# Gate and up weights loaded in eighths, transposes in quarters, the down groups regrouped, and three step counts moved

## The chip, the cores and the metric

The kernel runs on one core of one Trainium2 chip. A time is the device time of one whole execution in microseconds (us); lower is better. The profile was taken on one execution of its own. Engines are named as the profile names them: PE is TensorE (matmuls, with its weight loads as PEld), DVE is VectorE, ACT is ScalarE, POOL is GpSimd, SP is SyncE, which here issues every DMA of the program from one in-order queue.

## What is computed

One transformer layer over 2048 rows of width 512, everything in fp32, with 32 heads of width 16 that share one key and one value head, and a gated linear unit of inner width 1792:

```python
mod = (silu(c) @ w_mod).reshape(1, 6, 1, 512)       # sa, ca, ga, sb, cb, gb
h = layernorm(x) * (1 + ca) + sa
q, k, v = h @ wq, h @ wk, h @ wv                    # q: 32 heads of 16; k and v: one head of 16
o = softmax(q @ k.T / 4) @ v                        # for each head
x = x + ga * (o @ wo)
h = layernorm(x) * (1 + cb) + sb
x = x + gb * ((sigmoid(h @ w_gate) * (h @ w_up)) @ w_down)
```

Products of activations with weights are made from fp16 pairs: each fp32 operand is split into a high and a low half, and three matmuls (high by high, high by low, low by high) stand for one.

## The kernel before

**Units and half-steps.** A prologue normalizes x and makes k, v and a first part of q. Then come 32 attention units. A unit is one block `b` of 256 rows (8 blocks) and one group `o` of 8 heads (4 groups). It runs 16 steps `kb`, one for each 128 keys, and every step has two half-steps, `n` = 0 and 1; `s` = 16 times the unit plus `kb` counts steps through the program. A half-step issues, in a fixed order on PE, 8 score matmuls `sa` for a later unit (DVE takes row maxima `mx` of two 128x512 tiles from them), 8 score matmuls `st` (ACT makes two tiles `P` of exponentials) and 4 fp32 matmuls that add P times V into `craw`. After them `piece(s, n)` issues a piece of other PE work, if the plan has one: a slice of a q, wo, gate/up or down product.

**The other work.** Once the four units of a block are done, the block's feed-forward part (`ffn_block`) becomes available: one `wo` couple (attention output times wo, `wo_group`), seven gate/up couples `gu_group` (one for each chunk of 256 of the 1792 inner columns), and two down couples `down_group`. A couple is two products, one for each 128 rows, whose matmuls alternate between the two halves of PE's rows. A gate/up couple has 192 matmuls of 64x32 by 512 columns, a `piece` carries 8 or a multiple of it (mostly 16 or 24). `plan` takes the next couple from the list `work` when the last one is used up; `pick` holds the head of the list back until what it needs has been transposed (`marks`) plus `GAP` = 2 steps; `pace` sets how many terms go into a half-step, between 2 and 3 for these couples, from what is left and the steps until it is due. Nothing overtakes the head of the list. The two down couples of a block cover the 14 inner slices as 8 (`HF`) and 6, and their order in the list is: six gate/up couples, the first down couple, the seventh gate/up couple, the second down couple. The `wo` couple of a block is urgent: from step 9 of the unit that follows the block's last one it goes ahead of whatever is left in the list, once the couple under way has ended.

**The chain from wo to gate.** When a wo product ends, `norm` (deferred by 1 step for the first 128 rows and 3 for the second) adds the residual on POOL; `norm2`, 2 steps later, makes mean and variance on DVE and 7 POOL instructions of the normalization (`row_norm`); `norm3`, 1 step later, scales and shifts on POOL and splits into the pair `h2r`; 3 steps later (`HLATE`) SP issues a DMA transpose of 8 blocks of 128x128 that makes `h`, and sets the mark. Gate/up couples have a like chain: ACT (`th`) and DVE or ACT (`u`) evict, POOL makes `gr` in 4 instructions (`gated_rows`), 3 steps later (`GLATE`) SP transposes it to `g`, which the down couples read.

**Weights.** The gate and up weights are split once into fp16 pairs by `weight_jobs` (a DMA of 256 KB to `wst`, three POOL instructions) and stored to `wD` in DRAM, seven chunks of 1 MB. Jobs for wo, gate/up and the first 10 slices of w_down (42 in all) are spread over `WSTEPS` = 90 steps; the last four, whose place in SBUF the q weights hold, follow from step 100. Each gate/up couple needs its chunk back in SBUF as `gw`, of which there are two buffers; `ask` issues the load of the chunk after, one DMA of 1 MB, when a couple begins.

**Also on SP,** once in a unit: two DMAs `lD<-cs`, eight `raw<-cs`, `lc<-lD`, six `qp<-qD`, `lD<-rc` and `raw<-lD` (they carry the softmax sums to and fro and place the attention output by rows, so that POOL can make `a`, which wo reads), and four `qp<-mh`. What is pinned runs on each engine in the order in which the code issues it; only the tail, after the last unit, is ordered by a scheduler.

Of the kernel before, what the change touches and what calls it, by code (L numbers as in the profile page):

```python
# [16 lines left out]
P = 128  # L17
# [10 lines left out]
NDC = D // P  # L28
# [33 lines left out]

SKIP = 9
GAP = 2
CHAIN = 26
QRATE = 1.1
MOST = 3
# [1 line left out]
HELD = 60  # L69
SWAP = 5  # L70
FRESH = 0.9
WSTEPS = 90
WLAST = 100
WLATE = 2
WSTORE = 5
# [13 lines left out]
NCH = F // 256  # L89
# [3 lines left out]
def adaln_mqa_glu_kernel(  # L93
# [133 lines left out]
    def pair(name):  # L227
        return wp.tile([P, 2, 512], F16, tag="f16", name=name, bufs=HBUFS)
# [24 lines left out]
    sp1 = Ordered(nc.sync)  # L253
# [500 lines left out]
    now = [0]  # L754

    def defer(n, f_):
        waits.append((now[0] + n, f_))

    WO = {}
    wD = dr.tile([NCH, P, NDC, 4, 256], F16, name="wD")  # L760
    CH = [*range(2, NCH), 0, 1]
    FS = [2 * c_ + e for c_ in CH for e in range(2)]

    def gw_tile():
        return P2.tile([P, NDC, 4, 256], F16, tag="gw", name="gw", bufs=GWB)
# [26 lines left out]
    tail = []  # L792

    marks = {}

    use, gws = [0], {}

    def ask(upto):
        while use[0] <= upto:
            k = use[0]  # L800
            gws[k] = gw_tile()
            sp1.dma_start(gws[k], wD[CH[k % NCH]])
            use[0] += 1

    def ffn_block(b, end_of_all=False):
        x1, xrs, h2, ups, ths, gT = {}, {}, {}, {}, {}, {}
        at = b * NCH
        HF = 8

        def wo_group(t):  # L810
            def term(n, rs):
                o, i = divmod(n, 3)
                a_, w_ = passes(*aTs[b, o], WO['woh'], WO['wol'])[i]
                return a_[rs, t * P:(t + 1) * P], w_[rs, o, :]

            def begin():
                xrs[t] = t32("xr")
                sp1.dma_start(xrs[t], x[b * QU + t * P:b * QU + (t + 1) * P, :])

            def end(po, second):  # L820
                xr, t1 = xrs.pop(t), t32("t1")
                if second:
                    act.activation(t1, po, AF.Identity)
                    pool.tensor_tensor(t1, t1, mods[2], op=ALU.mult)
                else:
                    dve.tensor_tensor(t1, po, mods[2], op=ALU.mult)
                if tail:
                    dve.tensor_tensor(xr, t1, xr, op=ALU.add)
                    row_norm([t1], [xr])
                    dve.tensor_tensor(t1, t1, mods[4], op=ALU.mult)  # L830
                    dve.tensor_tensor(t1, t1, mods[3], op=ALU.add)
                    x1[t] = xr, t1
                else:
                    defer(1 + 2 * t, lambda: norm(t, t1, xr))

            return Group("wo", 12, "po", term, end, begin)

        def norm(t, t1, xr):
            pool.tensor_tensor(xr, t1, xr, op=ALU.add)
            defer(2, lambda: norm2(t, t1, xr))  # L840

        def norm2(t, t1, xr):
            row_norm([t1], [xr], later=True)
            defer(1, lambda: norm3(t, t1, xr))

        def norm3(t, t1, xr):
            x1[t] = xr, t1
            pool.tensor_tensor(t1, t1, mods[4], op=ALU.mult)
            pool.tensor_tensor(t1, t1, mods[3], op=ALU.add)
            rows = pair("h2r")  # L850
            pool.tensor_scalar(rows[:, 0], t1, 1.0, 0.0, op0=ALU.mult, op1=ALU.add)
            pool.tensor_tensor(rows[:, 1], t1, rows[:, 0], op=ALU.subtract)
            h2[t] = turned(rows, f"h2{t}")
            if b == 0 and t == 0:
                ask(0)
            defer(HLATE, h2[t][1])

        def turned(rows, name):
            t_ = pair(name).rearrange("p a (c r) -> p (a c) r", r=P)

            def go():
                sp1.dma_start_transpose(t_, rows.rearrange("p a n -> p (a n)"))
                marks[b, name] = now[0]

            return t_, go

        def gu_group(c_, t):
            def begin():
                if t == 0:
                    ask(at + c_ + 1)  # L870
                    ths[c_], ups[c_] = t32("th"), t32("u")

            def term(n, rs):
                k, i = divmod(n, 3)
                gw = gws[at + c_]
                h_, w_ = ((0, 0), (1, 0), (0, 1))[i]
                return h2[t][0][rs, 4 * h_ + k, :], gw[rs, k, 2 * w_:2 * w_ + 2, :].rearrange("p m n -> p (m n)")

            def end(p_, second):
                ts = slice(256 * t, 256 * (t + 1))  # L880
                th, u_ = ths[c_], ups[c_]
                if second:
                    dve.tensor_copy(u_[:, ts], p_[:, 256:])
                    act.activation(th[:, ts], p_[:, :256], AF.Tanh, scale=0.5 / (SH * SW))
                else:
                    act.activation(th[:, ts], p_[:, :256], AF.Tanh, scale=0.5 / (SH * SW))
                    act.activation(u_[:, ts], p_[:, 256:], AF.Identity)
                if t == 1:
                    gated_rows(c_)

            return Group("gu", 12, "pgu", term, end, begin)

        def gated_rows(c_):
            th, u_ = ths.pop(c_), ups.pop(c_)
            pool.tensor_scalar(th, th, 1.0, 1.0, op0=ALU.add, op1=ALU.mult)  # L895
            pool.tensor_tensor(th, th, u_, op=ALU.mult)  # L896
            rows = pair("gr")
            pool.tensor_scalar(rows[:, 0], th, 1.0, 0.0, op0=ALU.mult, op1=ALU.add)
            pool.tensor_tensor(rows[:, 1], th, rows[:, 0], op=ALU.subtract)  # L899
            gT[c_], go = turned(rows, f"g{c_}")  # L900
            if tail:
                go()
            else:
                defer(GLATE, go)

        def gu_cols(c_, m):
            def begin():
                if m == 0:
                    ask(at + c_ + 1 if c_ < NCH - 1 else at + c_)

            def term(n, rs):
                e, (k, i) = n // 12, divmod(n % 12, 3)
                gw = gws[at + c_]
                h_, w_ = ((0, 0), (1, 0), (0, 1))[i]
                return gw[rs, k, 2 * w_ + m, e * P:(e + 1) * P], h2[k][rs, h_, :QU], lambda z: z[:, e * QU:(e + 1) * QU]

            def end(p_, second):
                if m == 0:
                    ths[c_] = th = t32("th")
                    act.activation(th, p_, AF.Tanh, scale=0.5 / (SH * SW))  # L920
                    return
                th, g_ = ths.pop(c_), pair("gc")
                dve.scalar_tensor_tensor(th, th, 1.0, p_, op0=ALU.add, op1=ALU.mult)
                pool.tensor_scalar(g_[:, 0], th, 1.0, 0.0, op0=ALU.mult, op1=ALU.add)
                pool.tensor_tensor(g_[:, 1], th, g_[:, 0], op=ALU.subtract)
                gT[c_] = g_

            return Group("gu", 24, "pgu", term, end, begin)
# [49 lines left out]
        gs = [Couple(gu_group(c_, 0), gu_group(c_, 1)) for c_ in range(NCH)]  # L978
        for g in gs:
            g.needs = [(b, "h20"), (b, "h21")]  # L980
        for ds in downs:
            gs.append(Couple(*ds))
            gs[-1].needs = [(b, f"g{c_}") for c_ in (range(HF // 2) if len(gs) == NCH + 1 else range(NCH))]
        gs.insert(NCH, gs.pop(NCH - 1))
        first = Couple(*wos)
        for g in [first, *gs]:
            g.b = b
# [13 lines left out]
    groups, rows = {}, []  # L1001
# [22 lines left out]
    for tok in PLAN.split():  # L1024
        name = tok.rstrip("0123456789")
# [23 lines left out]
    work, urgent = early, []  # L1049
# [23 lines left out]
    def pick(s):  # L1073
        if urgent and s >= urgent[0].ready:
            return urgent.pop(0)
        if work and all(k in marks and s >= marks[k] + GAP for k in getattr(work[0], "needs", ())):
            return work.pop(0)

    def pace(s, g):
        if g.stage == "q":  # L1080
            return QRATE, 2
        now_, late = s // (NU * NKB), s % (NU * NKB) >= CHAIN
        until = 2 * ((now_ + late) * NU * NKB + CHAIN)
        left = sum(z.n for z in [g, *urgent, *work] if late or z.b < now_ - 1 or z.stage == "wo") + 24 * late
# [33 lines left out]
    def piece(s, h):  # L1118
        plan(s, 2 * s + h)
        if run:  # L1120
            g, n0, n1 = run.pop(0)
            if n1 > n0:
                g.part(n0, n1)


    vq = []
# [2 lines left out]
    for i, (b, o) in enumerate(units):  # L1129
# [5 lines left out]
        for kb in range(NKB):  # L1135
            s = i * NKB + kb
# [12 lines left out]
            for n in range(2):  # L1149
                t = kb - kb % 2 + n  # L1150
                for z in ORDER:
                    k = int(z[1:] or 0)
# [14 lines left out]
            while wdone < nw:  # L1167
                if wdone < nw - 4 and (wdone + 0.5) * WSTEPS > (s + 1) * (nw - 4):
                    break
# [9 lines left out]
    while waits:  # L1179
        now[0] += 1  # L1180
        for z in [z for z in waits if z[0] <= now[0]]:
            waits.remove(z)
            z[1]()
    psum["ctx"].close()
    psum["ctx"] = ctx.enter_context(ExitStack())
    psum["b"] = psum["ctx"].enter_context(tc.tile_pool(name="pz", bufs=1, space=PSUM, reuse_waits="tile"))
# [47 lines left out]
```

## Time and profile before

| | |
|---|---|
| three runs | 1678.07, 1681.4, 1688.73 us, median 1681.4 |
| the profiled execution | 1682.25 us, its span 1680.5 us |
| PE busy | 1608.2 us, 96% of the span |
| DVE, ACT, POOL busy | 84%, 78%, 40% |
| units 0 to 3 (no feed-forward work yet) | 107.8 to 276.8 us |
| the first feed-forward couple | in unit 4, from about 305 us |
| the tail behind the last unit | about 1585 to 1680.5 us |

Times in the trace count from the start of the span. Busy is the time in which an engine has an instruction under way. A row of a view by stretches gives, for each engine, busy us and in brackets the number of instructions, then the clock that was granted to PE as a share of full speed. In a list of waits a row reads: engine, what waited, what it waited for, us in total, times, the longest one; "issue" is time for which the profile shows no releaser. In a list in order of time a bracket at the end gives the idle time before an instruction and who ended it; SPq are the DMA issues of SP.

### The profile page before, as it was taken

What the parts mean: (1) busy time and instruction counts of PE and PEld (TensorE: products, weight loads), DVE (VectorE), ACT (ScalarE), POOL (GpSimd) and SP (SyncE); (2) the same over time, 40 slices, a digit from 0 to 9 for tenths busy, and PEclk for the clock granted to TensorE, in tenths of its full rate; (3) what the DMA queues carried; (4) which work ended last, traced back from release to release, by engine and by line L of the source; (5) the groups of instructions that cost most, each with busy time, mean ns of one, the idle gap of its engine ahead of it and who ended that gap; (6) DMA issues with size and microseconds to landing.
All of it is one profiled execution on the core that took longest, in us unless ns stands there. A gap on an engine that the chain in (4) does not pass through costs nothing.

```text
span 1680.5 us, 91637 instructions
## 1 busy us (share of the span) xinstructions
PE 1608.2 (96%) x41477; PEld 991.0 (59%) x41477; DVE 1419.8 (84%) x2400; ACT 1305.5 (78%) x2409; POOL 666.2 (40%) x827
## 2 busy tenths in 40 slices
PE   6999999979999999999999999999999999999998
PEld 3335554436666566666566666666666666665465
DVE  7789999879999899999899999999899989993041
ACT  5549998768888888888888888888888888888600
POOL 4433756664315322362316331453226232442222
PEclk9989999989999999999999999999999999999999
DMA  7121433334321432233321341223322341233322
GB/s 243 57 69 43 126 130 125 93 99 127 85 59 28 113 81 52 57 89 84 78 59 35 116 104 24 59 86 83 82 59 65 84 103 54 29 112 83 108 76 75
DMA packets 145090, 140.18 MB, mean 83 GB/s; under 512 B 91332, under 2 KB 125116, under 8 KB 136636
## 3 DMA queue, kind: packets, MB, share of 16 engines
q1 hardware_dynamic: 144700, 134.32, 29.2%
q8 instruction: 325, 5.32, 1.3%
q14 instruction: 65, 0.53, 0.1%
HBM read 97.18 MB, written 16.24 MB: 67 GB/s over the span
## 4 chain that ended last, share of the span: by engine, by line
PE 81%; POOL 5%; ACT 4%; DVE 4%; DMA 3%; issue 2%; SPq 2%; POOLq 0%; ACTq 0%
PE craw L139 22%; PE pgu L139 17%; PE sa L139 16%; PE st L139 9%; PE pd L139 7%; PE po L139 3%; PE pgu L190 2%; PE pd L190 2%; PE pq L139 2%; DVE mx L139 2%; ACT P L139 2%; SPq L139 1%; POOL t L363 1%; DMA h<-h2r 1%; DMA xall<-in_A_x_dram 1%
## 5 line engine op out<-in xcount | busy, mean ns | idle before, releaser
L139 DVE TENSOR_REDUCE mx<-sa 128x1 f32<-128x512 f32 x2048 | 1310.0, 684 | 111.8 <-PE sa L139 56.3
L139 ACT ACTIVATE P<-st 128x512 f32<-128x512 f32 x2048 | 1180.5, 598 | 230.8 <-PE st L139 174.4
L139 PE MATMUL craw<-P,V 64*32 64x512 f32 x8192 | 1090.6, 598 | 2.1 <-issue 1.2
L139 PE MATMUL st<-qp,kp 64*32 64x512 f16 x8192 | 837.1, 380 | 11.3 <-ACT P L139 7.2
L139 PE MATMUL sa<-kp,qp 64*32 64x512 f16 (+1 forms) x7940 | 830.9, 379 | 8.9 <-DVE mx L139 5.5
L139 PEld LDWEIGHTS <-kp 64*32 64x32 f16 x8192 | 325.9, 91 | 262.5 <-issue 101.3
L139 PE MATMUL pgu<-gw,h 64*32 64x512 f16 x9408 | 422.2, 378 | 21.9 <-DMA h<-h2r 11.4
L139 PEld LDWEIGHTS <-qp 64*32 64x32 f16 (+1 forms) x7940 | 273.3, 92 | 139.7 <-issue 57.0
L139 PEld LDWEIGHTS <-h 64*32 64x32 f16 (+1 forms) x9600 | 211.8, 92 | 107.0 <-issue 41.7
L139 PEld LDWEIGHTS craw<-P,V 64*32 64x32 f32 x8192 | 194.8, 105 | 24.2 <-issue 5.1
L895 POOL TENSOR_SCALAR th<-th 128x512 f32<-128x512 f32 x49 | 30.3, 618 | 368.7 <-ACT th L139 242.6
L139 PE MATMUL pd<-wdh,g 64*32 64x512 f16 x2688 | 132.8, 377 | 0.8
L563 POOL MEMSET qp<- 32x1024 f16 x60 | 56.7, 944 | 131.7 <-PE st L139 129.7
L139 PEld LDWEIGHTS <-g 64*32 64x32 f16 x4032 | 86.7, 92 | 33.9 <-issue 6.7
L139 PE MATMUL pd<-wdl,g 64*32 64x512 f16 x1344 | 80.1, 376 | 0.0
L896 POOL TENSOR_TENSOR th<-th,u 128x512 f32<-128x512 f32 x49 | 62.9, 1284 | 4.1
L333 POOL TENSOR_SCALAR wst<-wst 128x512 f32<-128x512 f32 x46 | 28.4, 618 | 86.3 <-DMA wst<-in_B_w_gate_dram 28.8
L139 DVE COPY u<-pgu 128x256 f32<-128x256 f32 x49 | 20.3, 415 | 49.8 <-PE pgu L139 22.5
L948 POOL TENSOR_TENSOR ot<-ot,gb 128x512 f32<-128x512 f32 x12 | 15.4, 1282 | 115.9 <-ACT ot L139 115.9
L899 POOL TENSOR_TENSOR gr<-th,gr 128x512 f16<-128x512 f32 x49 | 57.1, 1164 | 4.0
L139 PE MATMUL craw<-nought 64*32 64x1 f16 x353 | 57.8, 164 | 0.0
L139 PE MATMUL pq<-h,wdh 64*32 64x512 f16 (+1 forms) x688 | 53.8, 386 | 0.1
(156 smaller groups left out, 1139.0 us busy)
## 6 DMA issues: line engine op xcount, KB each, us to landing
gw<-wD SPq DMA_DIRECT2D x56, 1024.0 KB
wD<-gw SPq DMA_DIRECT2D x7, 1024.0 KB
wm<-in_w_mod_dram SPq DMA_DIRECT2D x6, 1024.0 KB
qp<-qD SPq DMA_DIRECT2D x192, 32.0 KB
qD<-q SPq DMA_DIRECT2D x16, 256.0 KB
xr<-in_A_x_dram SPq DMA_DIRECT2D x16, 256.0 KB
out_dram<-ot SPq DMA_DIRECT2D x16, 256.0 KB
raw<-cs SPq DMA_DIRECT2D x248, 16.0 KB
```

Of the source, the lines that this page charges most:

```text
L139: return (lambda *a, **k: keep(f_(*a, **k))) if pinned else f_
L190: pe.matmul(cut[0](self.bank) if cut else self.bank, l_, r_, start=(n == 0), stop=(n == self.n - 1))
L333: pool.tensor_scalar(w_, w_, SW, 0.0, op0=ALU.mult, op1=ALU.add)
L363: eng.tensor_scalar(dst, src, mv[:, i, 0:1], rs[:, i:i + 1], op0=ALU.subtract, op1=ALU.mult)
L563: eng.memset(qp[j:j + 32], 0.0)
L895: pool.tensor_scalar(th, th, 1.0, 1.0, op0=ALU.add, op1=ALU.mult)
L896: pool.tensor_tensor(th, th, u_, op=ALU.mult)
L899: pool.tensor_tensor(rows[:, 1], th, rows[:, 0], op=ALU.subtract)
L948: pool.tensor_tensor(ot, ot, mods[5], op=ALU.mult)
```

## The change

Five things change; no arithmetic does.

1. `ask` no longer issues one load of 1 MB for a chunk but puts eight loads of 128 KB into a list; `turned` likewise makes four transposes of 2 blocks from one of 8. `drip`, called behind every `piece`, issues one part of them in a half-step, transposes first. `fetched` issues at once what is still missing of the chunk when its couple begins. The mark of a transposed tile is set with its last quarter.
2. A block's list is now seven gate/up couples and then the two down couples, which cover 6 and 8 slices.
3. `norm` is deferred by 1 and 2 steps in place of 1 and 3, and `norm3` follows `norm2` at once.
4. The first gate/up couple of block 0 waits 6 steps (`EGAP`) behind its mark in place of 2.
5. The 42 weight jobs are spread over 66 steps in place of 90.

```diff
+EGAP = 6
-WSTEPS = 90
+WSTEPS = 66
...
+    turns, loads = [], []
+
+    def drip():
+        if turns:
+            turns.pop(0)()
+        elif loads:
+            loads.pop(0)[1]()
+
+    def fetched(upto):
+        while loads and loads[0][0] <= upto:
+            loads.pop(0)[1]()
+
     def ask(upto):
         while use[0] <= upto:
             k = use[0]
-            gws[k] = gw_tile()
-            sp1.dma_start(gws[k], wD[CH[k % NCH]])
+            gws[k] = gw = gw_tile()
+            for z in range(NDC):
+                for y in range(2):
+                    at = slice(2 * y, 2 * y + 2)
+                    loads.append((k, lambda gw=gw, k=k, z=z, at=at: sp1.dma_start(gw[:, z, at], wD[CH[k % NCH], :, z, at])))
             use[0] += 1
...
-        HF = 8
+        HF = 6
...
-                    defer(1 + 2 * t, lambda: norm(t, t1, xr))
+                    defer(1 + t, lambda: norm(t, t1, xr))
...
             row_norm([t1], [xr], later=True)
-            defer(1, lambda: norm3(t, t1, xr))
-
-        def norm3(t, t1, xr):
             x1[t] = xr, t1
...
+            of = rows.rearrange("p a n -> p (a n)")
+
+            def part(z):
+                sp1.dma_start_transpose(t_[:, 2 * z:2 * z + 2], of[:, 2 * z * P:2 * (z + 1) * P])
+                if z == 3:
+                    marks[b, name] = now[0]
 
             def go():
-                sp1.dma_start_transpose(t_, rows.rearrange("p a n -> p (a n)"))
-                marks[b, name] = now[0]
+                turns.extend(lambda z=z: part(z) for z in range(4))
...
             def begin():
                 if t == 0:
+                    fetched(at + c_)
                     ask(at + c_ + 1)
...
-        gs.insert(NCH, gs.pop(NCH - 1))
...
-        if work and all(k in marks and s >= marks[k] + GAP for k in getattr(work[0], "needs", ())):
+        if work and all(k in marks and s >= marks[k] + (EGAP if k == (0, "h21") else GAP) for k in getattr(work[0], "needs", ())):
...
             if n1 > n0:
                 g.part(n0, n1)
+        drip()
```

In the tail, where nothing drips, `gated_rows` and the column form of the gate (`gu_cols`) issue all parts at once.

The order of instructions shows where this moves things. First SP in block 1, around the transposes of its first and second gate/up results. `gw<-wD` are weight loads, `g<-gr` transposes; the rest belongs to the unit. Before:

```order
L139 DMA_TRANSPOSE g_15352<-gr 128x8x128
L139 DMA lc<-lD 128x16
L139 DMA qp<-qD 16x4x256 x6
L139 DMA gw<-wD 128x4096
L139 DMA lD<-rc 128x16
L139 DMA raw<-lD 128x1x256
L139 DMA_TRANSPOSE g_15884<-gr 128x8x128
L139 DMA gw<-wD 128x4096
L139 DMA qp<-mh 1x16x64 x4
```

After:

```order
L140 DMA_TRANSPOSE g_15389<-gr 128x2x128 x2
L140 DMA lc<-lD 128x16
L140 DMA_TRANSPOSE g_15389<-gr 128x2x128 x2
L140 DMA qp<-qD 16x4x256 x6
L140 DMA gw<-wD 128x512 x5
L140 DMA lD<-rc 128x16
L140 DMA gw<-wD 128x512 x2
L140 DMA raw<-lD 128x1x256
L140 DMA_TRANSPOSE g_15959<-gr 128x2x128 x4
L140 DMA gw<-wD 128x512 x9
L140 DMA qp<-mh 1x16x64 x4
```

One load and one transpose have become runs of parts that stand between the unit's own DMAs.

Second DVE where block 1 ends and block 2 begins. `ot<-pd` ends the second down couple of block 1, `COPY u<-pgu` the first gate/up couple of block 2; two `mx` stand for a half-step. Before:

```order
L139 TENSOR_TENSOR ot<-pd,gb 128x512
L139 TENSOR_REDUCE mx<-sa 128x1 x8
L139 TENSOR_REDUCE m_21196<-mx 64x16 x2
L139 TENSOR_REDUCE mx<-sa 128x1 x8
L139 TENSOR_TENSOR mh<-m_21329,mh 32x64
L139 TENSOR_REDUCE mx<-sa 128x1 x14
L139 COPY u<-pgu 128x256
```

After:

```order
L140 TENSOR_TENSOR ot<-pd,gb 128x512
L140 TENSOR_REDUCE mx<-sa 128x1 x6
L140 TENSOR_REDUCE m_21418<-mx 64x16 x2
L140 TENSOR_REDUCE mx<-sa 128x1 x8
L140 TENSOR_TENSOR mh<-m_21548,mh 32x64
L140 TENSOR_REDUCE mx<-sa 128x1 x8
L140 COPY u<-pgu 128x256
```

Between the end of the last down couple and the end of the next gate/up couple there were 30 `mx`, 15 half-steps, and now there are 22, 11 half-steps, which is the length of the couple itself.

Third POOL in the first normalization, block 0, between the residual of the second 128 rows and the normalization of the first. `wst`, `wdh` and `wdl` are weight jobs. Before:

```order
L839 TENSOR_TENSOR xr<-t_7540,xr 128x512
L824 TENSOR_TENSOR t_7542<-t_7542,ga 128x512
L333 TENSOR_SCALAR wst<-wst 128x512
L839 TENSOR_TENSOR xr<-t_7542,xr 128x512
L334 TENSOR_SCALAR wdh<-wst 128x512
L563 MEMSET qp 32x1024 x2
L335 TENSOR_TENSOR wdl<-wst,wdh 128x512
L351 TENSOR_SCALAR ve<-mv 128x1
```

After:

```order
L855 TENSOR_TENSOR xr<-t_7568,xr 128x512
L840 TENSOR_TENSOR t_7570<-t_7570,ga 128x512
L855 TENSOR_TENSOR xr<-t_7570,xr 128x512
L564 MEMSET qp 32x1024 x2
L352 TENSOR_SCALAR ve<-mv 128x1
```

The weight jobs that stood among these instructions are all ahead of them.

More of the change, by code (lines that the diff above doesn't have):

```diff
@@ L900, in gated_rows @@
             gT[c_], go = turned(rows, f"g{c_}")
-            if tail:
-                go()
-            else:
+            if not tail:
                 defer(GLATE, go)
+                return
+            go()
+            while turns:
+                drip()
         def gu_cols(c_, m):
@@ L909, in begin @@
                     ask(at + c_ + 1 if c_ < NCH - 1 else at + c_)
+                    fetched(at + c_ + 1)
             def term(n, rs):
@@ L1123, in piece @@
                 g.part(n0, n1)
+        drip()
     vq = []
@@ L1183, in adaln_mqa_glu_kernel @@
             z[1]()
+    while turns or loads:
+        drip()
     psum["ctx"].close()
```

## The prediction

> **What bounds the kernel now.** I read the page first, then the span by stretches, the waits of the stretches in which PE stands, and in order of time what precedes the stands.
>
> ```profile
> span 1680.5 us, 91637 instructions
> PE 1608.2 (96%) x41477; PEld 991.0 (59%) x41477; DVE 1419.8 (84%) x2400; ACT 1305.5 (78%) x2409; POOL 666.2 (40%) x827
> ...
> q8 instruction: 325, 5.32, 1.3%
> ...
> gw<-wD SPq DMA_DIRECT2D x56, 1024.0 KB
> ```
>
> PE is the bound, with 72.3 us idle (1680.5 − 1608.2). The change takes no matmul away, so it can win idle time, or half-steps that are badly filled. Stretches (prologue left out): units 0 to 3, unit 4, unit 5 up to the first gate couple, that couple's start, the middle, the tail.
>
> ```profile
> core 0: us, PE busy (x) PEld busy (x) DVE busy (x) ACT busy (x) POOL busy (x), PEclk, DMA share, GB/s
> 107.80:276.80 169.00, 164.22 (x4057) 85.79 (x4050) 160.29 (x272) 150.90 (x276) 88.75 (x112) 0.98 0.31 98
> 276.80:322.60 45.80, 42.55 (x976) 21.37 (x976) 40.87 (x69) 36.98 (x69) 26.73 (x34) 0.96 0.39 123
> 322.60:348.10 25.50, 25.09 (x494) 10.18 (x498) 25.43 (x46) 22.52 (x41) 23.48 (x31) 1.00 0.42 102
> 348.10:364.60 16.50, 7.12 (x133) 3.16 (x130) 4.85 (x8) 3.93 (x7) 13.49 (x17) 0.69 0.33 105
> 364.60:1585.00 1220.40, 1195.87 (x34744) 780.10 (x34732) 1079.83 (x1793) 1034.77 (x1925) 442.22 (x517) 1.00 0.30 75
> 1585.00:1680.50 95.50, 85.59 (x582) 54.45 (x569) 23.51 (x44) 7.31 (x15) 24.77 (x26) 0.99 0.23 76
> ```
>
> The fourth row is the largest single loss: 9.38 us of 16.5 idle, and the granted clock down to 0.69. The middle has 24.5 us idle in 1220.4. Now three kinds of half-steps there: four without other work, seven with 16 matmuls of it, and six with 24, 24, 16, 24, 16, 24.
>
> ```profile
> 918.76:923.70 4.94, 4.62 (x107) 2.15 (x87) 4.94 (x9) 4.59 (x9) 4.77 (x5) 1.00 0.27 51
> 955.90:965.09 9.19, 9.19 (x291) 6.16 (x285) 8.87 (x15) 8.15 (x15) 3.90 (x6) 1.00 0.54 163
> 897.96:906.75 8.79, 8.79 (x283) 6.48 (x278) 8.43 (x15) 7.09 (x13) 5.92 (x10) 1.00 0.15 37
> ```
>
> An empty half-step takes 4.94 / 4 = 1.235 us with DVE busy all of it; one of 16 takes 1.313, one of 21.3 (the six) 1.465. So 4 more matmuls cost 0.152 / 1.33 = 0.114, and the 16 alone 0.456: an empty half-step wastes 1.235 − (1.313 − 0.456) = 0.38 us.
>
> **First gate couple (parts 3, 4, 5).** PE's and DVE's waits between 348 and 365, POOL in block 0 and in block 1, and the chain:
>
> ```profile
> PE pgu L139 <- DMA h<-h2r: 9.4, 1, 9.4
> DVE mx L139 <- PE sa L139: 10.8, 4, 9.7
> ...
> 324.51 1.28 POOL L839 TENSOR_TENSOR xr<-t,xr 128x512 f32<-128x512 f32 x1
> ...
> 331.76 1.16 POOL L335 TENSOR_TENSOR wdl<-wst,wdh 128x512 f16<-128x512 f32 x1
> ...
> 354.53 1.15 POOL L852 TENSOR_TENSOR h2r<-t,h2r 128x512 f16<-128x512 f32 x1
> ...
> 355.71 3.02 DMA h<-h2r
> ```
> ```profile
> 522.99 1.28 POOL L824 TENSOR_TENSOR t<-t,ga 128x512 f32<-128x512 f32 x1 [4.90 <-ACT t L139]
> ...
> 545.82 1.17 POOL L852 TENSOR_TENSOR h2r<-t,h2r 128x512 f16<-128x512 f32 x1
> ```
>
> The couple was issued on PE before its `h` had landed at 358.7, and the attention matmuls queued behind it stood too. POOL needs 355.7 − 324.5 = 31.2 us for the two normalizations, against 547.0 − 523.0 = 24.0 in block 1, where no weight jobs stand among them. In the new order the jobs are gone from this place. The second 128 rows start a step earlier, `norm3` a step earlier: I put `h2r` at 345 to 349 on the old axis and `h` at 348 to 352. The order puts the couple at half-step 28 of unit 5, formerly 20; eight half-steps at 1.235 behind 348.1 make 358.0. So the couple no longer waits, by some 6 us. The 16.5 us held three half-steps of 44 matmuls each (133 in the row), which cost 8.79 / 6 = 1.47 each elsewhere: **−12.0**. DVE, now busy 4.85 of 16.5, is not late for anything behind. At worst, if `h` came only at 358, a wait of a few tenths is left; at best the slow clock behind the stand goes too (nothing more is counted).
>
> **Regrouping (parts 2 and 4).** By the instruction order the empty half-steps past the first gate are now 26 (four at the end of each of blocks 1 to 6, two in the last unit) and become 9 (two in unit 9, seven in unit 31), plus the eight of unit 5: 17. Nine fewer by 0.38: **−3.4**, of which I take −3, since the same matmuls also fill some half-steps from 16 to 24 at the price above.
>
> **Unit 4 (part 5).** A weight job waits for its DMA on POOL; `a` is behind it, PE's `po` behind `a`:
>
> ```profile
> 307.32 0.62 POOL L333 TENSOR_SCALAR wst<-wst 128x512 f32<-128x512 f32 x1 [1.50 <-DMA wst<-in_B_w_down_dram]
> 308.02 0.40 POOL L720 TENSOR_SCALAR a<-raw 128x256 f16<-128x256 f32 x1
> ```
> ```profile
> 308.47 0.41 PE L139 MATMUL po<-woh,a 64*32 64x512 f16 x8 [2.49 <-POOL a L720]
> ```
>
> With the 42 jobs ended at step 66 (unit 4 begins with step 64) this goes, 1.5 to 2.5 us; of the row's idle 3.25 us more than that can't go. I take **−2.5**. The price is in units 0 to 3: 64 of 66 steps' jobs instead of 64 of 90, 40.7 against 29.9, some 11 more at 0.62 + 0.62 + 1.16 = 2.4 us: POOL from 88.75 to 115 of 169 us, 68%. DVE is busy 160 of the 169 and sets the pace, so POOL's work lies beside it; only waits like the one above cost. Bounds 0 and eleven times 1.1 (12); nearest to the first, since 30 such jobs left PE idle only 4.78 us in that row: **+1**.
>
> **Loads and turns in parts (part 1).** PE's waits in the middle, with the largest one and its surroundings on SP and the DMA engines (the 5.6 us before it, then the 2.8 us with it):
>
> ```profile
> PE pgu L139 <- issue: 7.0, 8, 1.9
> PE st L139 <- issue: 4.0, 4, 2.1
> PE sa L139 <- issue: 2.9, 3, 1.5
> ...
> PE craw L139 <- issue: 1.2, 2, 0.9
> PE pgu L139 <- DMA h<-h2r: 2.0, 2, 1.3
> ```
> ```profile
> 816.49 0.38 SPq L139 DMA_DIRECT2D gw<-wD  x1
> 820.13 1.23 SPq L139 DMA_TRANSPOSE g<-gr  x1
> ```
> ```profile
> 823.44 0.37 PE L139 MATMUL st<-qp,kp 64*32 64x512 f16 x1 [2.09 <-issue]
> ```
> ```profile
> q1 hardware_dynamic: 433, 1.19, 58.6%
> ```
> ```profile
> q1 hardware_dynamic: 1075, 0.28, 86.6%
> q8 instruction: 1, 0.02, 2.1%
> ```
>
> 15.1 us in 17 waits have no releaser. In the 5.6 us in which a 1 MB load runs no instruction block (q8, 16 KB each by the page: 5.32 MB in 325) is moved; the first one comes with the transposes behind, and PE goes on after it. I read these waits as PE out of instructions, its block queued behind large transfers. Parts of an eighth let a block pass between them, so most go: −13, ends 0 and −15.1 (with the two `h<-h2r` waits −17).
>
> What the parts cost: 7 x 56 = 392 more loads at 0.38 on SP are 149 us, 3 x 63 = 189 more transposes between nothing (1.23 / 4 each) and 1.23 each 0 to 232. Spread over some 1300 us this is 11 to 29% of SP, beside PE, unless somebody waits. That is where parts are late: a couple takes about 11 half-steps, and 8 + 4 parts want 12; in the new order 30 of the 49 gate couples in the units begin by issuing one to three loads at once. Only the last terms need those slices, about 4 half-steps later, 5.3 us. Where SP is just then in one of its runs, this is exceeded:
>
> ```profile
> 810.41 4.00 SPq L139 DMA_DIRECT2D qp<-qD  x6
> ...
> 523.08 5.56 SPq L139 DMA_DIRECT2D raw<-cs  x8
> ```
>
> A run of 5.56 and a landing of some 2.5 (my estimate, below the 3.02 of `h`) less 5.3 make 2.8 us of PE. The order shows three starts right behind such a run (units 7, 30, 31); ends 0 and 3 x 2.8 = 8.4, I take **+3**, so part 1 gives **−10** in all.
>
> The Trainium skill ("DMA: Bandwidth & Descriptors", "Bandwidth") asks for transfers of at least 1 MiB and has 64 KB at 0.95 us and 1 MB at 6.15. By these figures an estimate for a chunk in eighths is over 7.6 us of the engines in place of 6.15, 1.45 more; were nothing of it hidden, the 30 starts named above would cost 44 us more and the time be 1695. The trace speaks against that: the middle row has the DMA engines 30% busy, and the leeway is 5.3 us.
>
> **Tail.** The first down product has 36 matmuls where it had 48, the second 48:
>
> ```profile
> 1616.01 0.44 PE L967 MATMUL pt<-ident,t 128*128 128x128 f32 x2 [1.24 <-DVE t L831]
> 1630.05 15.94 PE L190 MATMUL pgu<-h2c,gw 128*128 128x256 f16 x144 [1.76 <-DMA gw<-wD]
> ```
>
> Both waits, 3.0 us, can go as the last chunk's load and the last norm stand earlier; the work stays. Ends 0 and −4; **−3**.
>
> **Sum:** −12.0 − 3 − 2.5 + 1 − 10 − 3 = −29.5, so 1682.25 becomes 1652.8; the profiled execution was 0.85 above the median, which makes **1652** for a median.
>
> **Rivals.** *The blocks' waits don't depend on the loads' size.* For it: the wait above ends behind a transpose, not the load, and as many bytes go as before. Against it: before both stood a stretch without any block. It leaves 0 to −2 of −13 and the +3: 1663 to 1665, say **1664**. The Trainium skill ("Runtime: NRT & Kernel Launch", "Instruction fetch mechanics") calls the cost of a block's border mostly hidden; by that rule the 15.1 us would have another cause and this rival would hold, and the rows bear it out for most of the 325 blocks, not for the 17 waits.
>
> *POOL is late in units 0 to 3.* Eleven more jobs each hold POOL for a DMA as at 307.32, and the q that unit 1 to 4 need come late: the +1 becomes +12, **1663**. Against it: 68% busy leaves room.
>
> *Late parts make it slower.* At each of the 30 starts the last slices wait in SP's one queue, behind the unit's own DMAs and the turns, which go first, and PE, in order, stands with all its attention work behind. Without part 1's other effects the sum is −32.5 (−29.5 less the +3); from 1.08 us a start on there is no gain, from 1.65 on it is over 1% slower; at the 2.8 of a long run, all 30 make +84 and **1733**, 21 of them 1708. For it: `loads` give way to `turns`, and both to the unit's runs. Against it: most starts stand where SP's issues are short, and the leeway of 5.3 us is longer than a landing.
>
> **How the numbers follow.** The forecast's own range, 1652 ± 11, adds its ends: instruction waits −4 or +10, late parts −3 or +5, tail −1 or +3, units 0 to 3 by some. Chances: forecast 0.55, first rival 0.23, POOL 0.10, late parts 0.12 (half of it a partial loss near no change, half over 1% slower). One per cent, about what a measurement of this kernel can tell from no change, is 1664.6 and 1698.2. Below 1664.6 lie 0.52 of the forecast, 0.13 of the first rival and 0.06 of POOL: 0.71; slower 0.06; the rest 0.23. The range 1640 to 1674 holds the forecast but for 0.03, and the first two rivals with 10 us above them but for 0.03; it leaves out 0.18 with late parts.
>
> **What would show it.** The wait `pgu <- DMA h<-h2r` of 9.4 gone and eight empty half-steps of 1.24 ahead of the first gate couple; `po` in unit 4 without its 2.49; PE's "issue" waits past the first gate at 2 us instead of 15.1; `pgu <- DMA gw` at 3 us, in units 7, 30 and 31; POOL at 115 us in units 0 to 3 with PE's idle there near 5. I am wrong if the issue waits stay, or if `pgu <- DMA gw` has many entries of 1 us and more.

## The result and the profile after

The changed kernel takes 1739.37 us in the median of four runs (1735.77 to 1744.67) against 1681.1 for the kernel before: a ratio of 1.0342, with a 95% interval of 1.0298 to 1.0386. It is slower by 58 us, outside the range of 1640 to 1674 and on the side to which the forecast gave 0.06. The page of the profile after:

```profile
span 1742.9 us, 92267 instructions
...
PE 1630.9 (94%) x41482; PEld 991.7 (57%) x41482; DVE 1421.3 (82%) x2400; ACT 1303.3 (75%) x2409; POOL 666.0 (38%) x827
...
gw<-wD SPq DMA_DIRECT2D x448, 128.0 KB
```

PE is idle for 112.0 us in place of 72.3, and busy for 22.7 us more with the same matmuls (five small ones more on record). The waits of PE over the whole span (engine, what waited, for what: us in total, times, longest) name the first of the two:

```profile
PE pgu L140 <- DMA gw<-wD: 66.8, 22, 7.3
...
PE pgu L140 <- DMA h<-h2r: 6.2, 5, 1.9
...
PE st L140 <- issue: 0.3, 1, 0.3
```

Before the change the couples in the units never waited for `gw`; now 22 waits take 66.8 us. The "issue" waits, 15.1 us before, are down to 0.3. The stretches with the same borders in the program as in the prediction's table, except that unit 5 now runs without work up to its 28th half-step (unit 5 up to the first gate couple, then the middle with that couple's start, then the tail, here from the start of the last half-step, which lay at 1583.9 us before):

```profile
core 0: us, PE busy (x) PEld busy (x) DVE busy (x) ACT busy (x) POOL busy (x), PEclk, DMA share, GB/s
105.10:277.30 172.20, 167.63 (x4051) 85.79 (x4044) 161.71 (x272) 150.59 (x276) 116.20 (x148) 0.97 0.39 124
277.30:318.90 41.60, 40.66 (x984) 21.74 (x978) 40.62 (x70) 36.94 (x69) 12.76 (x17) 1.00 0.16 47
318.90:355.50 36.60, 36.03 (x702) 14.78 (x709) 36.43 (x66) 32.55 (x61) 22.87 (x30) 1.00 0.24 59
355.50:1649.10 1293.60, 1214.16 (x34641) 779.41 (x34625) 1073.73 (x1781) 1026.05 (x1911) 443.42 (x518) 0.97 0.28 72
1649.10:1742.90 93.80, 86.68 (x593) 54.76 (x592) 23.90 (x44) 8.24 (x16) 23.93 (x24) 1.00 0.25 75
```

Ahead of the fourth row things went near the forecast: the first gate couple no longer stands, unit 4 is 4.2 us shorter, and units 0 to 3 are 3.2 us longer. The loss lies in the middle alone: 1293.6 us, with 79 us of idle PE and a mean granted clock of 0.97.

How one of the long waits comes about is seen in SP's list in order of time, in unit 19:

```profile
1014.09 1.06 SPq L140 DMA_DIRECT2D gw<-wD  x2
1015.25 3.45 SPq L140 DMA_TRANSPOSE g<-gr  x2
1018.74 0.59 SPq L140 DMA_DIRECT2D lc<-lD  x1
1019.43 3.33 SPq L140 DMA_TRANSPOSE g<-gr  x2
1022.81 2.92 SPq L140 DMA_DIRECT2D qp<-qD  x6
1025.78 2.80 SPq L140 DMA_DIRECT2D gw<-wD  x6
```

```profile
1028.92 0.63 PE L140 MATMUL pgu<-gw,h 64*32 64x512 f16 x8 [7.29 <-DMA gw<-wD]
```

SP has no pause from 1014 to 1028.6. Four quarter transposes take 6.8 us of it, the unit's own six loads of `qp` 2.9, and only behind these come six eighths, of which the first four are the missing half of the chunk that PE is working on. Its couple began on PE at 1018.0, and PE has been standing since 1021.6.

The same happens at each late start. Set side by side in time, 14 of the 49 gate/up couples began on PE with three or four of their eight loads still unissued; SP issued these 2.8 to 10.2 us behind the start, and all 14 couples stood, eight of them twice. Three more had one load left, issued within 1.1 us, and no couple but the 14 stood. PE came to the first slice that it lacked 3.5 to 5.8 us behind the start, after 48 or 64 of the couple's 192 matmuls, and from the issue of that slice to the end of the stand it took 2.6 to 3.7 us. Issued at the start, the slice would have been there when PE came, or nearly (an estimate from these two spans): the late issue makes the wait, not a slow landing. What a transpose costs SP is told by the list of its own instructions (count, then shortest, median and longest in ns), of the kernel before and of the changed one:

```profile
L139 SPq DMA_TRANSPOSE g<-gr x49: 1232/1270/2675, 382.7 to 1586.3; - x49
```

```profile
L140 SPq DMA_TRANSPOSE g<-gr x196: 1167/1237/2984, 380.4 to 1650.8; - x196
L140 SPq DMA_TRANSPOSE h<-h2r x56: 1167/1232/2563, 338.3 to 1527.2; - x56
```

A quarter holds SP nearly as long as a whole: 1237 ns against 1270. All DMA issues of SP between the starts of unit 6 and of the last half-step, added up from the trace, are 484 us of 1207 before and 935 of 1289 after.

The second part of the loss, PE's longer busy time, is in four stretches around the same wait:

```profile
1011.00:1021.60 10.60, 10.54 (x306) 6.67 (x302) 10.15 (x18) 9.19 (x19) 3.00 (x4) 1.00 0.26 57
1021.60:1028.90 7.30, 0.04 (x1) 0.00 (x0) 0.52 (x1) 0.51 (x2) 0.69 (x1) 0.83 0.38 95
1028.90:1034.20 5.30, 5.28 (x105) 2.64 (x112) 2.33 (x4) 1.91 (x4) 0.00 (x0) 0.59 0.57 155
1034.20:1040.00 5.80, 5.80 (x190) 3.69 (x178) 5.62 (x10) 5.17 (x9) 1.82 (x3) 1.00 0.26 59
```

In the 5.3 us behind the wait the granted clock is 0.59, which costs 5.3 x 0.41 = 2.2 us more. In the middle of the changed kernel the trace has the clock at 0.50 for 88.7 us, in 14 stretches of 3.4, 6.8 or 10.2 us, one at each of the 14 couples, beginning within the stand or up to 1.2 us behind it. While PE was busy this cost 34.7 us; before the change there is no such stretch in the middle. The Trainium skill ("TensorE: Matmul & The Clock Gate", "Part 1: The HAM clock gate") says that PE's clock is halved after an idle window of about 3.4 us and comes back after as long a busy one; this trace agrees at the stand of 7.3 us, with 0.50 from 1026.5 to 1033.3 us, but it also has 3.4 us at 0.50 behind a stand of only 1.9 us (at 389.1), and there the measurement decides.

### The profile page after: what moved, and what is told of

The parts are those of the page before. It is cut to its first block, busy times and chain, and to the rows that moved or that the text cites. A ratio compares the mean times of both kernels' runs of the same rounds, so it can differ in the third digit from the quotient of the medians.

```text
span 1742.9 us, 92267 instructions
## 1 busy us (share of the span) xinstructions
PE 1630.9 (94%) x41482; PEld 991.7 (57%) x41482; DVE 1421.3 (82%) x2400; ACT 1303.3 (75%) x2409; POOL 666.0 (38%) x827
## 4 chain that ended last, share of the span: by engine, by line
PE 69%; SPq 7%; issue 7%; DVE 5%; DMA 5%; POOL 4%; ACT 3%; POOLq 0%; ACTq 0%; DVEq 0%
PE craw L140 19%; PE sa L140 13%; PE pgu L140 12%; PE st L140 8%; SPq L140 7%; PE pd L140 6%; DVE mx L140 4%; DMA gw<-wD 3%; PE po L140 2%; PE pq L140 2%; PE pd L191 2%; PE pgu L191 2%; ACT P L140 1%; POOL th L915 1%; DMA h<-h2r 1%
## 5 line engine op out<-in xcount | busy, mean ns | idle before, releaser
L140 PE MATMUL craw<-P,V 64*32 64x512 f32 x8192 | 1109.0, 608 | 1.0 <-ACT cs L140 1.0
L140 PE MATMUL pgu<-gw,h 64*32 64x512 f16 x9408 | 431.6, 389 | 76.7 <-DMA gw<-wD 66.8
L140 PEld LDWEIGHTS <-qp 64*32 64x32 f16 (+1 forms) x7940 | 268.9, 93 | 140.8 <-issue 56.5
L140 PEld LDWEIGHTS <-h 64*32 64x32 f16 (+1 forms) x9600 | 216.4, 94 | 178.2 <-issue 119.2
L140 PEld LDWEIGHTS <-g 64*32 64x32 f16 x4032 | 84.9, 92 | 31.5 <-issue 6.6
L720 POOL TENSOR_TENSOR raw<-raw 128x256 f32<-128x256 f32 x31 | 22.7, 734 | 180.6 <-DMA raw<-lD 89.0
```

The costliest lines, as they stand in the source:

```text
L140: return (lambda *a, **k: keep(f_(*a, **k))) if pinned else f_
L720: keep(pool.tensor_tensor(raw[:, :QU], raw[:, :QU], raw[:, QU:], op=ALU.mult))
```

## The experiments

Theory T: the quarter transposes fill SP's one queue, so the last parts of a chunk are issued too late. Rivals: L, the eighths are late by themselves; P, the regrouped couples follow too closely for any load. Ratios are to the kernel before, in brackets the 95% interval; "SP" is the sum named above.

| kernel | transposes of, loads of | us | ratio | SP us | PE's waits for gw, us |
|---|---|---|---|---|---|
| changed | 2 blocks, 128 KB | 1739.37 | 1.0342 (1.0298 to 1.0386) | 935 | 66.8 |
| e1 | 8 blocks, 128 KB | 1635.65 | 0.9738 (0.9715 to 0.9762) | 694 | 0 |
| e2 | 2 blocks, 1 MB | 1672.2 | 0.995 (0.993 to 0.997) | 763 | 0 |
| e3 | 8 blocks, 1 MB | 1657.75 | 0.9864 (0.9835 to 0.9894) | 485 | 0 |
| e4, part 1 alone | 2 blocks, 128 KB | 1732.13 | 1.0314 (1.0286 to 1.0341) | 934 | 53.3 |
| e5 | 4 blocks, 128 KB | 1654.78 | 0.9819 (0.9776 to 0.9863) | 784 | 13.9 |
| e6, loads first | 2 blocks, 128 KB | 1689.76 | 1.0049 (1.0026 to 1.0072) | 937 | 0.3 |
| e7 | 2 blocks, 256 KB | 1672.73 | 0.993 (0.9896 to 0.9963) | 848 | 0 |
| e8 | 8 blocks, 256 KB | 1649.04 | 0.9794 (0.9767 to 0.9821) | 570 | 0 |

(Waits of the tail left out; a 0 means that no such wait was listed.)

**e1: whole transposes, the rest of the change.**

```diff
-                turns.extend(lambda z=z: part(z) for z in range(4))
+                sp1.dma_start_transpose(t_, of)
+                marks[b, name] = now[0]
```

> The changed kernel, but each transpose is one of 8 blocks again, issued at once; the loads stay in eighths. In the changed kernel's trace PE waits 66.8 us in 22 places for gw, and a quarter transpose holds SP for 1.42 us in the mean, as long as a whole one did (1.47). Theory T (the quarter turns fill SP's queue, so that the last eighths of a chunk are issued late): 183 transposes fewer in the units are some 240 us of SP less; the waits for gw fall under 8 us, the slow clock behind them goes, and the time is 1739 - 62 - 22 = about 1655 (1645 to 1668). Theory L (eighths dripped one a half-step are late by themselves): the waits stay above 40 us and the time above 1705. Theory P (the regrouped couples follow each other too closely for any load): as L.

The page and the stretch between the first gate couple and the tail:

```profile
span 1638.5 us, 92018 instructions
...
PE 1598.2 (98%) x41481; PEld 980.6 (60%) x41481; DVE 1414.9 (86%) x2400; ACT 1303.4 (80%) x2409; POOL 667.5 (41%) x827
```

```profile
354.60:1545.00 1190.40, 1183.76 (x34736) 770.21 (x34721) 1072.62 (x1792) 1030.73 (x1921) 445.71 (x521) 1.00 0.34 78
```

The waits for `gw` in the units are gone and PE is idle 6.6 us in 1190. T holds; L and P fall, for the loads in eighths and the couples' order are those of the changed kernel. Here too 12 couples begin with one to four loads unissued, but SP issues nearly all of these within 2 us (the latest 4.6 us) behind the start, and none stands: loads left over at a start cost time only where SP is behind with its queue. The time is 20 us below T's forecast of 1655, which counted the slow clock's cost from 22.7 us; the profiles show the whole: between this one and the changed kernel's lie 104.4 us, 71.7 of them idle (112.0 − 40.3) and 32.7 PE's longer busy time (1630.9 − 1598.2). The clock is at 1.00 throughout this stretch, so the second part is in the main the slow clock (34.7 us by the clock's own record). With e12 this is the fastest version found, 45 us below the kernel before.

**e2: loads of 1 MB, transposes in quarters. e3: both whole,** so that parts 2 to 5 are left.

```diff
-            for z in range(NDC):
-                for y in range(2):
...
-                    loads.append((k, lambda gw=gw, k=k, z=z, at=at: sp1.dma_start(gw[:, z, at], wD[CH[k % NCH], :, z, at])))
+            sp1.dma_start(gw, wD[CH[k % NCH]])
```

(e3 has the edit of e1 as well.)

> The changed kernel, but each chunk is loaded by one DMA of 1 MB again when the couple ahead of it begins; the transposes stay in quarters. T and L both: the load is issued 11 half-steps early, before most of the turns, so waits for gw fall under 10 us; T has SP still busy for over 700 us of the middle stretch, and waits for h or g after the last quarters of 5 to 15 us. PE's issue waits come back with the 1 MB loads, 8 to 15 us: about 1665 (1655 to 1680). P: the waits for gw stay above 30 us and the time above 1690.

> The changed kernel without part 1: loads of 1 MB and transposes of 8 blocks, as before the change; regrouping, norm steps, the later first gate and the earlier weights stay. T and L: the forecast's sum without part 1, 1681 - 19.5 = about 1662 (1654 to 1668), with issue waits near 15 us and no waits for gw. P: above 1690 with waits for gw.

PE's waits of e2, then of e3:

```profile
PE pgu L140 <- issue: 8.7, 9, 2.1
...
PE pgu L140 <- DMA h<-h2r: 4.9, 3, 2.8
PE st L140 <- issue: 4.3, 4, 1.3
PE sa L140 <- issue: 4.2, 3, 1.9
```

```profile
PE st L140 <- issue: 5.9, 5, 2.5
...
PE pgu L140 <- issue: 5.1, 7, 1.2
PE sa L140 <- issue: 2.7, 4, 0.9
PE craw L140 <- issue: 2.3, 2, 1.2
```

No waits for `gw` in either, and the issue waits are back with the 1 MB loads: 17.8 us (with 0.6 at `craw`) and 16.0. P is out. e3 agrees with the sum without part 1 as a whole: −23 measured, −19.5 forecast. From e3 to e1 eighths with whole transposes are worth 22 us, 14.3 of them issue waits (16.0 less 1.7). e2 against e3: the quarter transposes cost 14 us even where no load waits for them.

**e4: part 1 alone on the kernel before** (`EGAP`, `WSTEPS`, `HF`, the list and the norm steps as they were).

> The kernel before with part 1 alone: loads in eighths, transposes in quarters. T and L: a couple there has as few half-steps for 12 parts as in the changed kernel, save where the block's end has four empty half-steps, so the waits for gw are 40 to 70 us, the issue waits are gone, the first gate still stands for 9 us or more: 1681 + 30 to 75, about 1735. P: waits for gw under 15 us and a time below 1690.

```profile
PE pgu L140 <- DMA gw<-wD: 53.3, 16, 5.9
PE pgu L140 <- DMA h<-h2r: 9.3, 3, 5.5
```

As T expected: +51 us. The waits are 16 and not 22, but the couples that stand are again 14; fewer of them stand twice. The waits for `h` are the first gate couple's, 9.1 us in two.

**e5: transposes in halves.**

```diff
-                sp1.dma_start_transpose(t_[:, 2 * z:2 * z + 2], of[:, 2 * z * P:2 * (z + 1) * P])
+                sp1.dma_start_transpose(t_[:, 4 * z:4 * z + 4], of[:, 4 * z * P:4 * (z + 1) * P])
...
-                turns.extend(lambda z=z: part(z) for z in range(4))
+                turns.extend(lambda z=z: part(z) for z in range(2))
```

> The changed kernel with two transposes of 4 blocks in place of four of 2; loads in eighths. If a transpose holds SP for 1.4 us whatever its size, SP is busy for about 697 + 61 x 1.42 = 785 us of the middle stretch (697 with whole turns, 883 with quarters), and a couple has 10 parts in its 11 half-steps, so that few starts have parts to issue at once. Theory T1 (the parts that are left over at a start are what costs): waits for gw below 10 us, 1640 (1635 to 1652). Theory T2 (any added SP work costs, in proportion): half of the way, or with two thirds of the 183 transposes saved a third of it: about 1670.

```profile
PE pgu L140 <- DMA gw<-wD: 13.9, 12, 2.9
```

SP's time came out as expected, 784 us, so a transpose's price hardly depends on its size between 2 and 8 blocks. The time lies between the theories: two thirds of the saved transposes give back, by the ratios, 88 of 102 us, more than in proportion, but 13.9 us of waits remain where T1 had below 10.

**e6: loads ahead of transposes in `drip`,** the same work on SP.

```diff
-        if turns:
-            turns.pop(0)()
-        elif loads:
-            loads.pop(0)[1]()
+        if loads:
+            loads.pop(0)[1]()
+        elif turns:
+            turns.pop(0)()
```

> The changed kernel, but a half-step issues a weight part first and a quarter transpose only where no weight part is left. SP's work is the same, 880 us of the middle stretch. T1: each chunk is asked for some 11 half-steps ahead and its 8 parts go out in the first 8 of them, so none is left at the next start: waits for gw below 10 us; the turns come up to 8 half-steps later, which only the down couples and the first gate couple of a block feel (some held half-steps): 1650 (1640 to 1668). T2: the waits stay at 40 us or more, whoever is named, and the time above 1700.

```profile
PE sa L140 <- DVE mx L140: 12.1, 6, 3.6
PE po L140 <- POOL a L721: 8.1, 3, 3.8
PE pgu L140 <- DMA h<-h2r: 6.7, 5, 2.4
PE st L140 <- DMA qp<-mh: 4.6, 2, 2.8
...
PE pgu L140 <- DMA gw<-wD: 0.3, 1, 0.3
```

T1 names the waits for `gw` rightly (0.3 us left), but its 1650 is missed by 40 us. The queue is still overfull, and others now stand in it. The largest wait, `sa` for `mx`, is one of them: in five of its six times DVE had stood 2.5 to 4.6 us for `lc`, which SP issues behind four turns (SP's list, then DVE's):

```profile
851.72 5.71 SPq L140 DMA_TRANSPOSE g<-gr  x4
857.47 0.58 SPq L140 DMA_DIRECT2D lc<-lD  x1
```

```profile
861.12 0.25 DVE L140 RECIPROCAL rc<-lc 128x16 f32<-128x16 f32 x1 [4.59 <-DMA lc<-lD]
```

`a`, which needs `raw` from SP, the rows `mh` and `h` are late as well; that SP is the reason there too is a reading. So both hold: loads left over behind a full queue make the longest waits, and with 937 us of work on SP something is late in either order.

**e7: quarter transposes, loads of 256 KB. e8: whole transposes, loads of 256 KB.**

```diff
-                for y in range(2):
-                    at = slice(2 * y, 2 * y + 2)
-                    loads.append((k, lambda gw=gw, k=k, z=z, at=at: sp1.dma_start(gw[:, z, at], wD[CH[k % NCH], :, z, at])))
+                loads.append((k, lambda gw=gw, k=k, z=z: sp1.dma_start(gw[:, z], wD[CH[k % NCH], :, z])))
```

(e8 has the edit of e1 as well.)

> The changed kernel with loads of 256 KB, four to a chunk; the transposes stay in quarters. T1: 4 + 4 parts in 11 half-steps leave none over: waits for gw below 15 us, 1655 (1640 to 1670). T2: SP has some 100 us less to do, 780 in all, as with half turns: the same time as that run, whatever it is. If an instruction block gets past a load of 256 KB as it does past 128 KB, the issue waits stay below 3 us.

> Whole transposes and loads of 256 KB, four to a chunk, for a version with less SP work than the one that was fastest so far (whole transposes, eighths, 1635.65). Waits for gw stay below 3 us. If issue waits depend on a load's size alone, between none at 128 KB and 16 us at 1 MB, 2 to 4 us of them come back: 1638 (1633 to 1645).

e7, then e8:

```profile
PE pgu L140 <- DMA h<-h2r: 6.4, 4, 3.0
PE pgu L140 <- issue: 5.9, 8, 1.5
PE st L140 <- DMA qp<-mh: 5.1, 3, 3.2
...
PE sa L140 <- issue: 2.3, 5, 0.7
```

```profile
PE pgu L140 <- issue: 2.5, 5, 0.8
PE st L140 <- issue: 1.8, 3, 1.3
...
PE craw L140 <- issue: 1.4, 3, 0.7
PE sa L140 <- issue: 1.1, 2, 0.7
```

Both are slower than expected (1655 and 1638). e7 has no loads left over at any start and no waits for `gw`, but SP has 848 us of work and not the 780 expected, and `h` and `mh` are late, as they are in e6. The issue waits at 256 KB are 9.1 (with 0.9 at `st`) and 6.8 us, against 0 to 1.6 at 128 KB and 15 to 17 at 1 MB (all from 300 us on, ahead of the first load of `gw`): they grow with the load's size. e8 has less SP work than e1 and is slower by 0.0056 of the time before, 9 us; between the profiles lie 7.4 us, of which 4.5 are idle and 2.9 longer busy time.

**The other parts, each undone on e1.** Their ratios are to other runs of the kernel before than e1's, so differences from e1 go by the ratios. e9: `HF` and the list as before. e10: `WSTEPS = 90`. e11: `EGAP = 2`. e12: `norm` and `norm3` as before.

```diff
-        HF = 6
+        HF = 8
...
+        gs.insert(NCH, gs.pop(NCH - 1))
```

> Whole transposes, loads in eighths (1635.65 so far), with the block's list as before the change: down couples of 8 and 6 slices, the first ahead of the seventh gate couple. The forecast's term for the regrouping, -3 us from nine empty half-steps fewer, would bring 1639. But by its order of instructions this kernel has no empty half-step behind the first gate at all, since the closer norm steps alone remove the ones at the blocks' ends: then 1636 (1632 to 1640), and the regrouping is worth nothing beside the norm steps.

> Whole transposes, loads in eighths, the weight jobs spread over 90 steps again. By the forecast's terms: the po wait of 2.5 us in unit 4 comes back, units 0 to 3 win 1 us (by the traces of the four runs so far 2 to 4 us, 169.0 against 171 to 173), and the first h is up to 7 us later than now (its second transpose is issued at 347.5 us of 323.5 for unit 5, the first gate couple stands in the order at about 354), so that the first gate couple waits 0 to 5 us. 1638 (1633 to 1645).

> Whole transposes, loads in eighths, the first gate couple 2 steps behind its mark, which is half-step 16 of unit 5 in place of 24, some 10 us earlier. The second transpose of h is issued at 347.5 us and lands 3 us later at 350.5, the couple would come at about 344: PE stands 6 to 7 us there, the clock drops behind it, and eight half-steps of work stand 10 us earlier, worth 8 x 0.38 = 3 us later. If the later gate is worth what the forecast says, 1640 (1637 to 1645); if it only moves the wait elsewhere, 1636.

> Whole transposes, loads in eighths, norm deferred by 1 and 3 steps and norm3 a step behind norm2 as before the change. By the order of instructions the first gate couple stands 4 half-steps later (5 us, with h later by as much) and two empty half-steps in unit 9 and two more in unit 31 come: 8 x 0.38 = 3 us, 1639 (1635 to 1644). If the closer steps matter more for h's landing in the later blocks, waits for h of 5 us or more: above 1644.

| undone | us | ratio |
|---|---|---|
| regrouping (e9) | 1683.47 | 0.9998 (0.9983 to 1.0013) |
| weights in 66 steps (e10) | 1643.83 | 0.9763 (0.9737 to 0.9788) |
| later first gate (e11) | 1643.24 | 0.9763 (0.9733 to 0.9792) |
| closer norm steps (e12) | 1636.95 | 0.9723 (0.9696 to 0.975) |

PE's waits of e9, of e10 and of e11:

```profile
PE pgu L140 <- DMA h<-h2r: 23.1, 6, 4.2
```

```profile
PE pgu L140 <- DMA h<-h2r: 5.2, 1, 5.2
```

```profile
PE pgu L140 <- DMA h<-h2r: 5.5, 1, 5.5
```

e9 misses its expectation by 47 us and is 44 us slower than e1. Without empty half-steps at a block's end, the next block's first gate couple comes ahead of its `h`: one stand of 3.5 to 4.2 us in each of blocks 1 to 6, and at each the clock falls (at the second one 724.3 to 727.4):

```profile
724.30:727.40 3.10, 3.10 (x60) 1.31 (x52) 1.19 (x2) 0.98 (x2) 1.95 (x4) 0.50 0.73 230
```

By the pages, 31.8 us of its 47.6 over e1's profile are idle (72.1 − 40.3) and 15.8 are longer busy time (1614.0 − 1598.2). The six stands are 23.1 of the idle time; the tail is 7.5 us longer too. The order on PE shows what the regrouping does: in e1 a down couple of 384 matmuls and 31.5 us lie between the end of the `wo` couple and the first gate couple at that place, in e9 288 matmuls and 23.6 us, which is less than `h` needs. The stands come with the closer norm steps and the old list together: e12 (old steps, new list) doesn't have them, nor have the kernel before and e4 (old steps, old list, though with other transfers). e10 and e11 each bring back a wait of 5 us at the first gate couple, so each of the two parts keeps it away; in the time, 4 us each, neither differs from e1 by more than their intervals. e12 shows no difference: beside the regrouping no gain of the norm steps can be measured.

## Why the prediction was wrong

**The step that failed is the price of the parts on SP, the term of +3.** It stands against 66.8 us of waits for `gw` and 34.7 us of slow clock. With the 45 us that e1, without the quarter transposes, gains, these make +56; measured were +58. The forecast had the right mechanism as its third rival, and gave it 0.12. That the rival's 1733 lies near the 1739 measured is in part luck: it had 30 starts at 2.8 us and no slow clock, where 14 couples stood 4.8 us in the mean. In the term three things were wrong:

- It bounded a quarter transpose between a quarter of 1.23 us and all of it, up to 232 us more on SP. The upper end held: 48 + 12 whole transposes in the stretch from 364.6 to 1585 were 87 us before and 179 + 48 quarters 324 after, and with the loads SP's issues grew by some 450 us (484 to 935) where the two terms allowed 149 to 381. But it then judged SP by a share of the whole span, "11 to 29%". What counts is the queue within the 11 half-steps of one couple: four quarters in a row, 6.8 us in unit 19, make a run as long as the unit's longest (eight `raw<-cs`, 7.0 us there).
- It therefore priced late starts only right behind one of the unit's own long runs, and found three. Its sum for one start (run and landing, less the time until PE needs the slice), 2.8 us, was below the 4.8 measured (PE does not need the missing slices with its last terms alone, as the forecast had it), but the number of starts was further off, 3 for 14. The late ones were above all those at which PE stood in half-steps 13 to 15 (units 10, 11, 14, 15, 18, 19, 22, 23, 26, 27), where `raw<-cs`, four turns and `qp<-qD` follow one another: 53 of the 66.8 us. "Most starts stand where SP's issues are short" fits SP's list before the change, in which the turns were single, but not the one after.
- It had no term for the clock behind a stand, though the first row of loss that it read (0.69) held one.

**What held.** The first gate couple's wait is gone, at the place forecast (half-step 28, at 355.5 us; the forecast's 358.0 lay on the old axis, without unit 4's gain). POOL in units 0 to 3 has 116.20 us against 115 forecast; that stretch took 172.2 us where it took 169.0. It took 171.0 and 171.2 in e4 and e10, which have the old 90 steps, and 170.7 to 173.3 in all with 66, so that the weights cost 1 to 2 of it (an estimate from the means), forecast +1. The tail gave 2.7 of the 3 us (96.5 before, from the last half-step on). The issue waits went from 15.1 to 0.3 (forecast: 2 left), and they depend on the load's size, as the runs at 128 KB, 256 KB and 1 MB show: the first rival is out.

**What was sized wrongly without harm.** Unit 4 gave 4.2 us, forecast 2.5: the bound by its idle 3.25 us left out that its clock was 0.96 and is 1.00. The regrouping was priced by empty half-steps alone, −3; e9 shows that beside the closer norm steps it keeps six stands away, and is worth 44 us there. So e3's agreement with the sum says little of this term. What the regrouping is worth alone on the kernel before was not run.

**The Trainium skill's rule on large transfers** ("DMA: Bandwidth & Descriptors", "Bandwidth") didn't decide it: in e1 the same eighths make the kernel 22 us faster than loads of 1 MB. A sentence that speaks for the forecast, in the Trainium skill (the same page, "Issuing engines are not separate DMA queues"), says that the time the issuing sequencer takes is usually small beside the transfer; here it was what came late, with SP's issues at 935 of 1289 us and the DMA engines 28% busy.

## What to carry to other kernels

Cutting transfers into parts is priced on the queue that issues them, part by part and within the shortest period in which they must all be out, never as a share of the span; where a part costs the issuer as much as the whole (transposes here), cut only the ones that gain from it. A late transfer in front of an in-order engine cost its wait and, on PE here, some 2.5 us of slow clock for each couple that stood (34.7 us over 14). Before two edits are summed, ask whether one of them only works because of the other: the closer norm steps without the regrouping brought six stands and took back 44 us.

## What was not expected of the hardware

A transpose of 2, 4 and 8 blocks of 128x128 holds SP for 1.24, 1.23 and 1.27 us in the median. The waits of PE for which the profile names no releaser follow the size of the loads in flight: from 300 us on 15 to 17 us in the kernels with 1 MB, 7 to 9 with 256 KB, 0 to 1.6 with 128 KB. That they are waits for blocks of instructions is still a reading from which transfers stand side by side, and no run takes the blocks away. Over all runs, between the prologue and the tail, every stand of PE of 3.9 us or more (up to 9.4) came with a stretch at a clock of 0.50, none of those below 1.9 us did unless the clock was low already, and of those between some did: 1.9 us at 389.1 in the changed kernel, but not 3.8 us at 787.4 in e4.
